# A new order for the jobs of the first 45 attention steps and of the first wide pair in a fused threshold attention and ELU feed-forward kernel

## The chip, the cores and the metric

The kernel runs on one core of a Trainium2 chip. The metric is the device time of one execution in microseconds (us); several executions of a kernel are timed, and the median is used. A profile is one more execution, recorded by the hardware profiler; its span runs from the first to the last instruction on the core.

The core has five engines that run side by side, each with its own queue, in order: TensorE (PE in the profile: matrix products; PEld is its loading of the stationary operand), VectorE (DVE), ScalarE (ACT), GpSimd (POOL) and SyncE (SP, which here only starts transfers, called DMAs). An instruction that needs another engine's result waits for a semaphore, and everything behind it on its own engine waits with it.

## The reference

```
def _attn_ref(q, k, v, tau):               # q, k, v: 8 batches, 8 heads, 576 positions, 64 channels
    scale = 1.0 / np.sqrt(q.shape[-1])
    scores = scale * np.matmul(q, k.transpose(0, 1, 3, 2))
    thresh = np.max(scores, axis=-1, keepdims=True) - tau
    scores = np.where(scores >= thresh, scores, -1000000000.0)
    scores = scores - np.max(scores, axis=-1, keepdims=True)
    attn = np.exp(scores)
    attn = attn / (np.sum(attn, axis=-1, keepdims=True) + 1e-09)
    return np.matmul(attn, v).astype(np.float32)

x = attn_out.transpose(0, 2, 1, 3).reshape(4608, 512)
h = x @ w_in                               # w_in: 512 x 2048
g = np.where(h > 0.0, h, np.exp(np.minimum(h, 0.0)) - 1.0)
out = g @ w_out                            # w_out: 2048 x 512
```

All is in float32, except the two weight matrices, which come as float64 and are turned into float32 on the core.

## The kernel before

**The work.** Attention goes by pairs of heads, 32 pairs in all, four to a batch. A pair has five blocks of queries: four of 128 queries for both heads (i = 0 to 3), and a last one that holds the remaining 64 queries of both heads (i = 4, named NC in the code). One block of one pair is a step. The first 45 steps are numbered n = 0 to 44: steps 0 to 7 are blocks 0 and 1 of pairs 0 to 3, steps 8 to 19 are blocks 2, 3 and 4 of pairs 0 to 3, and then each of the pairs 4 to 8 has five steps in a row (pair 8: steps 40 to 44). They are built by `early_tasks`. From pair 9 on (`JOINED`) a different, wider form is used (`wide_step`, `tail_step`); pair 9 is the first wide pair, and its stage has the letter "j". The feed-forward layer fills PE between the attention's matmuls: two half batches in a plain form within the 45 steps (`ffn1`, `ffn2_plain`, called halves), and the rest in a form with seven products in place of eight (`first_product`, `second_round`) beside and after the wide pairs.

**One step** is a chain over four engines, for each head h:

- `sc`: PE computes the scores into a bank of PSUM (line 650).
- `max`: DVE takes the negated row maximum (line 707).
- Then one of two forms. The plain form: `th` is the threshold on POOL (line 711), `exp` is exp(score - max) on ACT (line 745), and `mask` on DVE multiplies it by score >= threshold and sums the row (line 752). The sunk form, for the (step, head) pairs in `MASK_ACT`: `th` is on DVE (line 723), `exp` is a Prelu with a slope of 2^126 on ACT that sends what is below the threshold far down (line 730), and `mask` is an exp on ACT with the row sum (line 736). The bank of scores becomes free behind `mask` in the plain form and behind `exp` in the sunk one.
- `su`, `rec`: the row sum on DVE (line 760) or, for the steps in `SU_ACT`, on ACT (line 697), and its reciprocal on DVE (line 766).
- `norm`: the weights are divided by their sum: on POOL (line 703), on ACT for `ACT_NORM` (line 691), on DVE for `NORM_DVE` (line 686).
- The weights are transposed in one of two ways. `part` and `put`: PE transposes into PSUM in two or three parts (line 769), and each is copied out by ACT or, for `PUT_DVE`, by DVE (line 785). Or, for the steps named by `SQUARES` (most of 22 to 44): `turned`, DVE transposes 32 x 32 squares (line 845), SP writes them to DRAM with four DMAs (line 870), and `landed` is the DMA that fetches them back in the right order (line 878 or 887).
- `val`, `out`: PE multiplies by the values for two or three steps of a pair at once (lines 902 and 907), and ACT copies the result out.

**Other jobs** stand between the steps: `load`, `v`, `loadr` (DMAs of q, k, v; `loadr` brings the last 320 positions of pair 0's q), `prep`, `scale`, `copy` (q and k are transposed by DVE, line 561 and 569, and q is scaled on POOL), `rest` with nothing behind it (the transposition of what `loadr` brought, on DVE), and for each of 32 pieces of the weights `lw` (its DMA), `shift` (DVE line 478, or POOL line 476 for `SHIFT_POOL`), `rest` (ACT line 469, or POOL line 489 for `REST_POOL`), `sign` (ACT line 494), `add` (POOL line 484) and `end` (DVE line 502), which turn float64 into float32. `in` makes sums of weight blocks for the seven-product form, on DVE or POOL (`IN_POOL`). `half` and `post` are the feed-forward halves and what follows them: exp on ACT, minus one on POOL, the ELU on DVE; for a unit in `ELU_ACT`, ACT also makes the relu, and POOL does the rest with two instructions.

**Idle transposes** are transposes of the identity whose result nobody reads. 22 run at the start (line 1309, `idle(22)`), 16 beside step 0 (line 1549, `idle(16)`), and `IDLES` holds triples (step, part, count): so many are issued ahead of that part of that step, in the same PSUM tile.

**What sets the order.** Nothing is scheduled by the compiler: instructions stand on each engine in the order in which the Python code issues them. Each job has a due time made of a formula, a shift from the table `MOVED` for its kind, and a shift from `MOVED` for this one job. Jobs are issued in the order of due time; a job that needs others issues those first.

```
    def task(x, t, key, f, *needed):
        each = "_".join(map(str, x)) if isinstance(x, tuple) else x
        made[x] = [t + (MOVED.get(key, 0.0) if key else 0.0) + MOVED.get(each, 0.0), len(made), f, needed, False]

    def do(x):
        job = made[x]
        if not job[4]:
            job[4] = True
            for y in job[3]:
                if y:
                    do(y)
            job[2]()
...
        for x in sorted(made, key=lambda x: made[x][:2]):
            do(x)
```

So a due time far behind (1100, say) only means that the job is issued when another needs it. In the wide pairs, posts stand on an agenda with due times of their own, shifted by `MOVED` under keys that begin with the stage's letter.

Of the kernel before, what the change touches and what calls it, by code (L numbers as in the profile page):

```python
# [18 lines left out]
ACT_NORM = {(1, 1), (4, 1), (8, 0), (8, 1), (10, 0), (11, 0), (11, 1), (13, 0), (14, 1), (15, 0), (16, 0), (17, 0), (18, 0),  # L19
 (18, 1), (20, 0), (20, 1), (21, 0), (21, 1), (25, 0), (26, 0), (29, 0), (30, 0), (31, 0), (35, 0), (36, 0), (37, 0), (38,  # L20
 0), (40, 0), (42, 1), (43, 0), (44, 0)}
IN_POOL = {(0, 0), (1, 0), (1, 2), (2, 2), (3, 1), (4, 0), (4, 1), (4, 2), (5, 1), (5, 2), (6, 0), (6, 1), (6, 2), (7, 1),
 (7, 2)}
SU_ACT = {0, 2, 5, 7, 16, 17, 20, 21, 23, 24, 25, 27, 30, 33, 37, 38, 43, 44}
QK_PE = set()
MASK_ACT = {(0, 0), (0, 1), (1, 1), (2, 0), (5, 1), (7, 1), (8, 0), (9, 1), (12, 1), (13, 0), (15, 1), (16, 0), (17, 1),
 (20, 0), (20, 1), (23, 0), (23, 1), (24, 0), (25, 0), (25, 1), (26, 0), (26, 1), (27, 0), (27, 1), (28, 0), (29, 0), (30,
 0), (31, 0), (32, 0), (32, 1), (33, 0), (33, 1), (35, 1), (36, 1), (37, 0), (37, 1), (38, 1), (39, 0), (40, 0), (41, 0),
 (42, 0), (44, 0)}
SHIFT_POOL = {0, 2, 3, 19, 23, 24, 26, 29}  # L30
REST_POOL = {0, 2, 3, 4, 5, 7, 11, 12, 13, 17, 24, 27, 30, 31}
IDLES = {(0, 1, 1), (1, 2, 2), (2, 0, 3), (2, 2, 2), (3, 0, 5), (3, 1, 3), (3, 2, 3), (5, 0, 6), (5, 1, 4), (6, 1, 6), (7,
 0, 2), (7, 1, 2)}
ELU_ACT = {(1, 0), (1, 2), (1, 3), (1, 4)}
NORM_DVE = {(1, 0), (12, 0), (19, 0), (23, 0), (23, 1), (27, 0), (30, 1), (32, 0), (32, 1), (33, 0), (34, 0), (35, 1), (36,
 1)}
WIDE_ACT = {(9, 1, 0), (9, 2, 1), (9, 4, 0)}
PUT_DVE = {(0, 2), (4, 2), (6, 2), (10, 1), (11, 0), (11, 1), (11, 2), (12, 0), (12, 1), (12, 2), (14, 0), (18, 1), (20, 1),
 (21, 0), (26, 2)}

MOVED = {
# [322 lines left out]
def kernel(  # L364
# [921 lines left out]
    def early_tasks():  # L1286
# [159 lines left out]
        for n in range(MIDDLE):  # L1446
# [9 lines left out]
            if n == LATE:  # L1456
                task("switch", t, None, switch, *rooms)
            rooms += [("exp" if (n, h) in MASK_ACT else "mask", n, h) for h in hs]
            at_ = (lambda a, b, c=0: t + c) if last_ else (lambda a, b, c=0: t + b) if late_ else (lambda a, b, c=0: t + a)
# [606 lines left out]
```

## Time and profile before

| what | us |
|---|---|
| median of 3 runs (lowest, highest) | 1289.68 (1289.25, 1290.15) |
| the profiled execution's own time | 1287.79 |
| its span | 1286.0 |
| granted clock of PE, mean | 0.999 |

The page gives, for each engine, the time in which it was busy, and for stretches of the span the same, with the granted clock of PE (1.00 is full speed) and the share of the 16 DMA engines that was in use. Two things are needed to read it. A matmul's record is longer than the distance to the next, since they overlap: a float32 matmul with 256 columns is two passes that each show about 380 ns, while the next pass starts 216 ns later. So "busy" on PE includes short waits; what PE really had to do is counted by the undisturbed distance between starts. And a wait for several semaphores is put down to the one that came last by the records, which can be the wrong one when a DMA is among them.

The 45 steps end at about 270 us: the last early instruction of PE starts at 269.28 us.

### The profile page before, as it was taken

The page shows a single profiled execution, that of the slowest core. Times are in us where ns is not written, and L with a number is a line of the kernel's source. Part 1 is how long each engine was busy: PE and PEld are TensorE (multiplying, and loading weights), DVE is VectorE, ACT ScalarE, POOL GpSimd, SP SyncE. Part 2 cuts the span into 40 slices and gives each one's busy share as a digit, 9 for nine tenths or more (in the row PEclk, how much of TensorE's full clock was granted, in tenths as well). Part 3 has the DMA queues.
Part 4 walks back from the last instruction along what each step waited for, and adds up shares of the span by engine and source line. Part 5 has one row for each costly group of instructions (what it writes and reads, how often), then busy time and mean ns, then how long its engine had stood idle before and what let it go on. Part 6 is the DMA issues. An engine that isn't in the chain of part 4 may idle for free.

```text
span 1286.0 us, 21531 instructions
## 1 busy us (share of the span) xinstructions
PE 1268.9 (99%) x6749; PEld 986.9 (77%) x6749; DVE 997.8 (78%) x2145; ACT 598.0 (46%) x1298; POOL 792.8 (62%) x1149
## 2 busy tenths in 40 slices
PE   8999999999999999999999999999999999999998
PEld 6675575467778787888888787878787888888887
DVE  6797777779798988898889888997989872545534
ACT  6889775555352526253535444443535251421320
POOL 4777566587476847675676657674758473534523
PEclk9999999999999999999999999999999999999999
DMA  7467687988989998998989898989898874222221
GB/s 140 137 179 166 160 246 210 240 236 246 238 227 267 246 240 231 236 256 228 248 229 271 214 238 216 260 223 242 235 254 248 242 214 174 76 74 65 92 62 33
DMA packets 329586, 258.35 MB, mean 201 GB/s; under 512 B 209536, under 2 KB 290432, under 8 KB 329472
## 3 DMA queue, kind: packets, MB, share of 16 engines
q1 hardware_dynamic: 327376, 256.50, 73.7%
q8 instruction: 53, 0.87, 0.3%
q10 hardware_dynamic: 2096, 0.48, 0.2%
q14 instruction: 61, 0.50, 0.1%
HBM read 167.12 MB, written 89.78 MB: 200 GB/s over the span
## 4 chain that ended last, share of the span: by engine, by line
PE 87%; DVE 4%; DMA 3%; SPq 1%; POOL 1%; ACT 1%; issue 1%; DVEq 0%; ACTq 0%; POOLq 0%
PE f L1793 30%; PE f L1653 29%; PE sc L954 7%; PE sc L1027 7%; PE f L1079 4%; PE sc L650 3%; PE pv L907 2%; PE rt L769 2%; DMA there<-x 1%; PE sc L1019 1%; PE f L1131 1%; PE sc L1014 1%; DVE mx L707 1%; DMA wst<-in_moe_w_out_dram 1%; SPq L528 1%
## 5 line engine op out<-in xcount | busy, mean ns | idle before, releaser
L703 POOL TENSOR_SCALAR w<-w,rs 128x576 f32<-128x576 f32 x152 | 122.6, 816 | 81.1 <-DVE rs L766 71.8
L961 DVE TENSOR_REDUCE mx<-sc 128x1 f32<-128x576 f32 x207 | 148.1, 749 | 27.5 <-PE sc L954 23.7
L981 ACT ACTIVATE w<-sc,mx 128x576 f32<-128x576 f32 x113 | 81.6, 740 | 114.8 <-DVE mx L961 98.0
L1653 PE MATMUL f<-xt,sw 128*128 128x256 f32 x512 | 124.2, 385 | 1.5 <-ACT g L1715 0.5
L1653 PE MATMUL f<-xt,w_in_sb 128*128 128x256 f32 x512 | 122.3, 381 | 0.5 <-ACT w L1667 0.5
L845 DVE STREAM_TRANSPOSE x<-w 128x512 f32<-128x512 f32 (+1 forms) x153 | 108.9, 744 | 14.9 <-POOL w L703 11.9
L973 POOL TENSOR_SCALAR th<-mx,ntau 128x2 f32<-128x2 f32 (+1 forms) x114 | 35.0, 307 | 131.9 <-DVE mx L961 131.9
L1653 PEld LDWEIGHTS f<-xt,sw 128*128 128x128 f32 x512 | 93.5, 190 | 22.2 <-issue 4.5
L1653 PEld LDWEIGHTS f<-xt,w_in_sb 128*128 128x128 f32 x512 | 96.2, 190 | 16.1 <-ACT w L1667 3.2
L1793 PE MATMUL f<-w_out_sb,g 128*128 128x256 f32 x448 | 107.1, 382 | 0.0
L1793 PE MATMUL f<-w_out_sb,s 128*128 128x256 f32 x448 | 107.0, 382 | 0.0
L1653 PE MATMUL f<-x,w_in_sb 128*128 128x256 f32 x448 | 105.9, 379 | 0.0
L1793 PE MATMUL f<-t,s 128*128 128x256 f32 x448 | 105.8, 379 | 0.0
L954 PE MATMUL sc<-kT,qT 64*128 64x448 f32 (+4 forms) x736 | 103.4, 416 | 0.0
L954 PEld LDWEIGHTS sc<-kT,qT 64*128 64x128 f32 x736 | 80.7, 186 | 25.2 <-issue 16.2
L1740 POOL TENSOR_TENSOR s<-g 128x256 f32<-128x256 f32 x104 | 80.7, 781 | 28.5 <-PE f L1793 20.1
L988 DVE SCALAR_TENSOR_TENSOR w<-sc,th,w 128x576 f32<-128x576 f32 x113 | 88.1, 809 | 10.2 <-ACT w L981 9.9
L1793 PEld LDWEIGHTS f<-w_out_sb,g 128*128 128x128 f32 x448 | 84.1, 190 | 14.0 <-issue 3.1
L1793 PEld LDWEIGHTS f<-w_out_sb,s 128*128 128x128 f32 x448 | 84.1, 190 | 13.6 <-issue 2.5
L1653 PEld LDWEIGHTS f<-x,w_in_sb 128*128 128x128 f32 x448 | 85.0, 190 | 11.8 <-ACT s L1667 0.3
L1793 PEld LDWEIGHTS f<-t,s 128*128 128x128 f32 x448 | 85.1, 190 | 11.6
L703 POOL TENSOR_SCALAR e<-e,rs 128x576 f32<-128x576 f32 x92 | 68.1, 744 | 34.9 <-DVE rs L766 33.6
(232 smaller groups left out, 2858.0 us busy)
## 6 DMA issues: line engine op xcount, KB each, us to landing
there<-x SPq DMA_DIRECT2D x444, 144.0 KB, 3.8
wTb<-there SPq DMA_DIRECT2D x58, 576.0 KB, 6.1
wTa<-there SPq DMA_DIRECT2D x53, 576.0 KB, 5.1
sw<-win_sums SPq DMA_DIRECT2D x62, 384.0 KB, 4.1
t<-wout_sums SPq DMA_DIRECT2D x45, 512.0 KB, 5.6
qm<-in_q_dram SPq DMA_DIRECT2D x124, 72.0 KB, 4.9
wst<-in_moe_w_in_dram SPq DMA_DIRECT2D x16, 512.0 KB, 4.6
vm<-in_v_dram SPq DMA_DIRECT2D x64, 128.0 KB, 4.0
```

Of the source, the lines that this page charges most:

```text
L650: nc.tensor.matmul(scs[h][:, a, :HALF], qs[r], kT[r, k0 : k0 + HALF], start=True, stop=True)
L703: nc.gpsimd.tensor_scalar(wv, wv, st["rs"][:, h : h + 1], 1.0, ALU.mult, ALU.mult)
L845: nc.vector.transpose(x[:, :, c0 : c0 + nc_], src.rearrange("p (c g n) -> p g c n", c=nc_, n=T))
L954: on_banks(nc.tensor.matmul(o, qT[r, i * P : (i + 1) * P], kT[r, k0 : k0 + n], start=True, stop=True, skip_group_check=True), o)
L961: on_banks(nc.vector.tensor_reduce(st["mx"][:, h : h + 1], st["sc", h], axis=AX.XY if i == NC else AX.X, op=ALU.max, negate=True), st["sc" ...
L981: on_banks(nc.scalar.activation(st["e", h], st["sc", h], AF.Exp, bias=st["mx"][:, h : h + 1]), st["sc", h])
L988: on_banks(nc.vector.scalar_tensor_tensor(st["e", h], st["sc", h], st["th"][:, h : h + 1], st["e", h], ALU.is_ge, ALU.mult, accum_out=st[" ...
L1027: on_banks(nc.tensor.matmul(o, vm[:, h, c], parts[part][:, g0:g1, h * (NC + 1) + c], start=False, stop=(c == NC - 1), skip_group_check=Tru ...
L1079: nc.tensor.matmul(loc["ph"][:, k], w_in_sb[:, j, ft * P : (ft + 1) * P], xts[g][:, j, hf * CT : (hf + 1) * CT], start=(j == 0), stop=(j = ...
L1653: nc.tensor.matmul(loc["banks"][place], left[:, j], right[:, j], start=(begins and j == 0), stop=(j == 1), skip_group_check=True)
L1740: engine.tensor_tensor(o, x, y, op)
L1793: nc.tensor.matmul(place(m), lhs, rhs, start=(begins and v == 0), stop=(v == RU - 1), skip_group_check=True)
```

## The change

Only tables change: which engine does a job for which step, how many idle transposes there are, and the due times. The sets, as they stand in the diff:

```diff
-ACT_NORM = {(1, 1), (4, 1), (8, 0), (8, 1), (10, 0), (11, 0), (11, 1), (13, 0), (14, 1), (15, 0), (16, 0), (17, 0), (18, 0),
- (18, 1), (20, 0), (20, 1), (21, 0), (21, 1), (25, 0), (26, 0), (29, 0), (30, 0), (31, 0), (35, 0), (36, 0), (37, 0), (38,
- 0), (40, 0), (42, 1), (43, 0), (44, 0)}
-IN_POOL = {(0, 0), (1, 0), (1, 2), (2, 2), (3, 1), (4, 0), (4, 1), (4, 2), (5, 1), (5, 2), (6, 0), (6, 1), (6, 2), (7, 1),
- (7, 2)}
-SU_ACT = {0, 2, 5, 7, 16, 17, 20, 21, 23, 24, 25, 27, 30, 33, 37, 38, 43, 44}
+ACT_NORM = {(4, 1), (8, 0), (8, 1), (10, 0), (11, 0), (11, 1), (12, 0), (13, 0), (14, 1), (15, 0), (16, 0), (17, 0), (18,
+ 0), (18, 1), (20, 0), (20, 1), (21, 0), (21, 1), (25, 0), (26, 0), (28, 1), (29, 0), (35, 0), (36, 0), (37, 0), (38, 0),
+ (40, 1), (42, 0), (42, 1), (43, 0), (44, 0)}
+IN_POOL = {(0, 0), (0, 1), (1, 0), (1, 1), (2, 0), (2, 2), (3, 2), (4, 2), (5, 2), (6, 1), (6, 2), (7, 0), (7, 1)}
+SU_ACT = {0, 2, 15, 16, 17, 20, 23, 24, 25, 27, 32, 33, 35, 37, 43, 44}
...
-SHIFT_POOL = {0, 2, 3, 19, 23, 24, 26, 29}
-REST_POOL = {0, 2, 3, 4, 5, 7, 11, 12, 13, 17, 24, 27, 30, 31}
-IDLES = {(0, 1, 1), (1, 2, 2), (2, 0, 3), (2, 2, 2), (3, 0, 5), (3, 1, 3), (3, 2, 3), (5, 0, 6), (5, 1, 4), (6, 1, 6), (7,
- 0, 2), (7, 1, 2)}
-ELU_ACT = {(1, 0), (1, 2), (1, 3), (1, 4)}
-NORM_DVE = {(1, 0), (12, 0), (19, 0), (23, 0), (23, 1), (27, 0), (30, 1), (32, 0), (32, 1), (33, 0), (34, 0), (35, 1), (36,
+SHIFT_POOL = {2, 3, 16, 21, 23, 24, 28, 29, 30, 31}
+REST_POOL = {0, 1, 2, 3, 4, 5, 7, 10, 11, 12, 13, 17, 18, 24, 26, 27, 28, 30, 31}
+IDLES = {(1, 2, 1), (2, 0, 2), (2, 2, 2), (3, 0, 3), (4, 2, 2), (5, 1, 3), (6, 1, 4), (6, 2, 1), (7, 0, 1), (7, 1, 1)}
+ELU_ACT = {(1, 0), (1, 4), (1, 5)}
+NORM_DVE = {(1, 0), (5, 1), (17, 1), (19, 0), (22, 0), (23, 0), (23, 1), (28, 0), (32, 1), (33, 0), (34, 0), (35, 1), (36,
  1)}
-PUT_DVE = {(0, 2), (4, 2), (6, 2), (10, 1), (11, 0), (11, 1), (11, 2), (12, 0), (12, 1), (12, 2), (14, 0), (18, 1), (20, 1),
- (21, 0), (26, 2)}
+PUT_DVE = {(0, 1), (4, 2), (6, 2), (10, 1), (11, 0), (11, 2), (12, 1), (12, 2), (14, 0), (16, 1), (18, 1), (20, 0), (21, 0),
+ (26, 2)}
```

`MASK_ACT` gains (15, 0), (30, 1), (31, 1), (34, 0), (38, 0), (43, 0) and loses (31, 0), (36, 1), (39, 0): 45 sunk heads, not 42. The triples of `IDLES` add up to 20, not 39; the 22 and the 16 stay.

In `MOVED`, nearly every single-job shift of the 45 steps differs (203 of `post`, 100 of `rest`, 81 of `max`, 80 of `exp` and so on), and 121 of the keys of stage "j"; the shifts by kind of job and the keys of the other wide pairs ("s", "f") are the same. A few of the lines:

```diff
-    "add_0": -0.9, "add_1": 12.1, "add_10": 607.6, "add_11": 274.8, "add_12": 709.4, "add_13": 511.6, "add_14": 334.2,
+    "add_0": -13.9, "add_1": 13.1, "add_10": 700.6, "add_11": 219.8, "add_12": 675.4, "add_13": 494.6, "add_14":
...
```

What the new due times do to the order of the instructions, as far as it is spoken of later: `loadr` stands on SP right behind the first `lw`, ahead of pair 1's q and k, instead of behind pair 2's k; on DVE, `shift` of piece 0 and the transposition of the rest of q stand ahead of `max` of step 1, instead of on POOL and behind `rec` of step 3; `prep` of pair 2's q stands ahead of `mask` (2, 1) instead of behind it; between `rec` of step 12 and `rec` of step 14 DVE has three jobs fewer, which ACT has; on SP, the four DMAs of pair 9's k stand behind the writes of `turned` 41 and ahead of `landed` 40 and 41, instead of ahead of `turned` 38. On PE the order of the steps' matmuls stays the same from step 10 on, but for some feed-forward halves that stand one place earlier or later; in steps 0 to 9 `part` (3, 2) stands ahead of the scores of step 5 and `part` (4, 0) behind them as before.

More of the change, by code (lines that the diff above doesn't have):

```diff
@@ L25 @@
-QK_PE = set()
[L26 to L29, printed above, removed]
-SHIFT_POOL = {0, 2, 3, 19, 23, 24, 26, 29}
-REST_POOL = {0, 2, 3, 4, 5, 7, 11, 12, 13, 17, 24, 27, 30, 31}
@@ new lines @@
+IN_POOL = {(0, 0), (0, 1), (1, 0), (1, 1), (2, 0), (2, 2), (3, 2), (4, 2), (5, 2), (6, 1), (6, 2), (7, 0), (7, 1)}
+SU_ACT = {0, 2, 15, 16, 17, 20, 23, 24, 25, 27, 32, 33, 35, 37, 43, 44}
+QK_PE = set()
+MASK_ACT = {(0, 0), (0, 1), (1, 1), (2, 0), (5, 1), (7, 1), (8, 0), (9, 1), (12, 1), (13, 0), (15, 0), (15, 1), (16, 0),
[3 rows of a table added]
+SHIFT_POOL = {2, 3, 16, 21, 23, 24, 28, 29, 30, 31}
+REST_POOL = {0, 1, 2, 3, 4, 5, 7, 10, 11, 12, 13, 17, 18, 24, 26, 27, 28, 30, 31}
+IDLES = {(1, 2, 1), (2, 0, 2), (2, 2, 2), (3, 0, 3), (4, 2, 2), (5, 1, 3), (6, 1, 4), (6, 2, 1), (7, 0, 1), (7, 1, 1)}
```

609 rows, old and new, of tables (MASK_ACT, MOVED) are left out of this document.

## The prediction

> **What bounds the kernel.** I read the busy times, then windows cut at step boundaries, then what DVE and PE wait for in each.
>
> ```profile
> PE 1268.9 (99%) x6749; PEld 986.9 (77%) x6749; DVE 997.8 (78%) x2145; ACT 598.0 (46%) x1298; POOL 792.8 (62%) x1149
> ```
>
> PE bounds the whole. But its records overlap, so "busy" hides short waits. Counted by undisturbed distances between starts (109 ns for a 128x128 transpose, 216 ns for each pass of 256 columns), PE has 1204.3 us of work in the span of 1286.0 and is idle for 81.7. The change can win only from this, and touches the first 312 us. By window (columns: us, then PE, PEld, DVE, ACT, POOL busy, PEclk, DMA share, GB/s):
>
> ```profile
> 13.60:52.40 38.80, 37.40 (x261) 25.22 (x260) 31.35 (x74) 32.73 (x65) 26.34 (x43) 1.00 0.62 141
> 52.40:85.40 33.00, 32.12 (x183) 23.68 (x182) 30.43 (x66) 27.48 (x57) 25.15 (x29) 1.00 0.54 154
> 85.40:226.00 140.60, 139.60 (x665) 87.96 (x664) 108.02 (x225) 104.57 (x220) 91.83 (x115) 1.00 0.75 197
> 226.00:272.00 46.00, 41.56 (x175) 20.36 (x174) 36.02 (x75) 25.39 (x51) 30.87 (x47) 1.00 0.89 243
> ```
>
> PE's own idle time in these is 9.0, 2.95, 11.95 and 10.67 us (8.4 before 13.6, 6.7 in 272 to 312, 32.0 behind). So in the first two rows other engines set the pace for part of the time, in the third PE does, and in the fourth the DMAs (share 0.89) hold it. In the first row DVE leads: ACT's exps start 0.03 to 0.1 us behind DVE's maxima, while DVE waits for 7.45 us in all, most of it for
>
> ```profile
> DVE mx L707 <- PE sc L650: 2.7, 3, 1.4
> DVE w L752 <- ACT e L745: 2.5, 3, 1.3
> ```
>
> The second row's DVE is the tightest of all: from 61.2 to 85.5 us I find no wait of DVE's.
>
> **The change, term by term.** Over all, at this trace's durations, PE loses 19 transposes x 109 ns = 2.07 us; ACT 2.07 net (five `rest` of weights go to POOL, 3.43; three more sunk masks come, 2.33); DVE 1.14 net; POOL gains 0.49. None of this is a gain by itself; what counts is where it stood.
>
> *1. Steps 0 to 10.* Two of DVE's waits get work:
>
> ```profile
> 11.13 0.76 DVE L707 TENSOR_REDUCE mx<-sc 128x1 f32<-128x576 f32 x1 [1.19 <-PE sc L650]
> ...
> 19.69 0.82 DVE L752 SCALAR_TENSOR_TENSOR w<-sc,th,e 128x576 f32<-128x576 f32 x1 [0.90 <-ACT e L745]
> ```
>
> Into the first gap (1.19) go `shift` 0 (0.43) and the rest of q (0.51), which stood at 25.69 in the chain; into the second (0.90) `prep` of pair 2's q (0.78), which stood ahead of `max` (3, 0). The first needs `loadr`'s data by 10.6. Its four issues now stand right behind the first `lw`, where SP is idle from 4.22 to 5.82; at this trace's 2.60 us for four they go out from about 4.2 to 6.8, and `qr` lands 2.6 us after issue (median): 9.4, some 1.2 early. Pair 1's q and k go out that much later less SP's 1.6 of idle time; k had about 1.0 to spare. I follow the chain by hand: `max` (3, 0) 21.12 to about 20.4; `max` (4, 0) 26.16 to 25.3; `sc` (6) 34.27 to 33.05; `max` (8, 0) 43.68 to 42.45; `sc` (10) 52.40 to 51.2. Against it stand 1.6 us more of DVE work by step 10 (`norm` (5, 1), `put` (0, 1), two row sums), inside the 7.45 of waits; if that cover were gone, each would push its successor by itself (0.16 to 0.68). The idle transposes are not added: the five ahead of `part` (3, 0) end at 26.64 where `norm` on POOL ends at 26.59, and behind the six ahead of `part` (5, 0) PE still waits 0.23; without them most of that time becomes a wait. **1.2 us**; ends 0 and 2.1 (all transposes on the path).
>
> *2. Steps 11 to 15.* `put` (11, 1) (0.68), `put` (12, 0) (0.68) and `norm` (12, 0) (0.52) leave DVE for ACT, 1.88 us where DVE has no wait; ACT is free for 1.61 of 76 to 80 us. DVE could come 1.88 earlier, but PE can give back only its idle time between `sc` (10) and `sc` (15), 3.06, less the third row's steady 8% (about 1.0). **1.4**; ends 0 and 1.9.
>
> *3. 85 to 226 us.* PE is at 92% of what it could do. Two waits stand out, each for a POOL copy: 0.74 us at
>
> ```profile
> 144.29 1.24 PE L650 MATMUL sc<-kT,qd 128*128 128x288 f32 x4 [0.57 <-POOL qd L603]
> ```
>
> and 0.44 at `sc` (25). POOL gets 1.7 to 2.8 more work ahead of them (`rest`, `shift`) and has 2.19 and 2.79 idle there; DVE loses two shifts. **0.5**; ends -1.0 (POOL's cover fails) and 1.2 (both waits go).
>
> *4. 226 to 272 us.* These two rows decide:
>
> ```profile
> 262.50 1.21 PE L650 MATMUL sc<-kT,qd 128*128 128x288 f32 x4 [1.03 <-DVE w L752]
> ...
> 267.12 0.67 PE L902 MATMUL pv<-wTa,vd 128*128 128x256 f32 x2 [1.70 <-ACT w L730]
> ```
>
> `sc` (44) waits for `mask` (43, 0) on DVE; sunk, its bank is free behind `exp` on ACT, so that 1.2 goes. But `val` (8, 0) comes next. The row blames ACT, whose instruction was long done; `landed` 41 was issued at 261.53 and took 5.5 to 267.0, so the DMA holds it, and whatever `sc` (44) wins is waited here instead. Ahead of that issue the change puts pair 9's four loads of k (2.03 us for four in this trace), where SP has 1.07 + 0.80 = 1.87 idle:
>
> ```profile
> 254.10 4.73 SPq L870 DMA_DIRECT2D there<-x  x8
> 259.90 0.34 SPq L878 DMA_DIRECT2D wTa<-there  x1
> 260.29 0.43 SPq L1044 DMA_DIRECT2D xtail<-xs  x1
> 261.53 0.32 SPq L878 DMA_DIRECT2D wTa<-there  x1
> ```
>
> So nothing is lost at that price, and 2.0 of issues leave the way of `turned` 38 and 39. **0.2**; ends -1.3 (nothing gained above, the loads slow the landing) and 1.2.
>
> *5. The first wide pair.* The same jobs at other times; its PE waits add to 3.5 us (0.3 to 0.7 each). No row prices a reorder, so **0**, ends -1.5 and 1.5. The ELU unit takes 0.59 from ACT and 2.55 from POOL and gives DVE 0.68, with no PE instruction, inside POOL's 38%: 0.
>
> Sum: 1.2 + 1.4 + 0.5 + 0.2 + 0 = 3.3 us. On the profiled execution 1287.79 - 3.3 = 1284.5; the median of the runs is 1.89 above that one, so **1289.68 - 3.3 = 1286.4**, 0.26% faster. About 0.2%, 2.58 us, can be told from no change.
>
> **Rivals.**
>
> *B, the gain is given back (1287.1 to 1292.3, likeliest 1289).* PE arrives earlier and waits for what has not moved: `val` (7, 0), (7, 1) and (8, 0) wait 0.98, 0.59 and 1.86 for DMAs with the DMA share at 0.89. For it: that row. Against it: SP's issues follow the engines, so DMAs of work that comes earlier also start earlier. The same result comes by the clock:
>
> ```profile
> 6.76:10.18 3.42, 1.81 (x12) 1.00 0.79 164
> 10.18:13.59 3.41, 3.41 (x14) 0.50 0.75 142
> 27.24:30.65 3.41, 3.31 (x20) 1.00 0.92 148
> ```
>
> (Columns: us, PE busy, PEclk, DMA share, GB/s.) A window with 1.81 us busy was followed by one at half clock. The thinnest later one is the third: 2.06 of work, 0.55 of it idle transposes. If it drops under the bar, the next runs at half: 2.71 of work there against 1.71 possible, 1.0 lost. One to three such windows leave a gain of 2.3 to 0.3.
>
> The Trainium skill (TensorE: Matmul & The Clock Gate, Part 4: PE-mode transpose) says that transposes do not count as work for the clock; by that, taking them away could cost no window, and this half of rival B would be empty. The trace speaks against it: 22 idle transposes from 1.48 us, and nothing else on PE, are followed by full clock at 6.76. The sum is 3.3 by either.
>
> *C, slower (1294.5).* The queue of SP: pair 9's loads stand ahead of `landed` 40 and 41. Issues of `turned` 39 took 2.45 and 1.91 us each (245.9, 248.9) when the queue was full. Four at 2.45 are 9.8, less 1.87 idle, 7.9 late, passed one for one to `val` (8, 0); less 3.1 gained ahead, 4.8 slower: 1289.68 + 4.8 = 1294.5. It makes the total slower from about 1.25 us an issue, and by over 0.2% from 1.9. For it: DMA at 0.89. Against it: pair 9's k took 0.5 an issue at 238.95 in the same stretch.
>
> **Chances.** Forecast 0.56 (1283 to 1287: terms 1 and 2 mostly there); B 0.24; C 0.20. Faster by over 0.2%: 0.56; within: 0.24; slower: 0.20. The favourable ends add to about 8 (2.1 + 1.9 + 1.2 + 1.2 + 1.5), 1281.8, rounded down for the runs' spread to 1281; above, B whole and C up to 1293.5, four fifths of its price.
>
> **What would show it.** DVE works on the rest of q before `max` (1, 0), with no wait for its DMA, and waits less than 7.45 us from 13.6 to 51; `sc` (10) starts near 51.2; `sc` (15) near 82.8 instead of 85.4; PEclk stays 1.00 behind 13.6; `sc` (24) and `sc` (25) wait under 1.18 together; `sc` (44) waits for nothing; pair 9's issues take 0.5 each and `val` (8, 0) starts near 264. Wrong it is if `loadr` lands behind 10.6 (term 1 goes), if PE finds ACT's `put` late at 76 to 82 (term 2), if half clock is granted anywhere behind 13.6 (B), or if `landed` 41 is issued later than 261.5 (C).

## The result, and the profile after

Five runs of each kernel on one chip: 1281.10 us (1280.39 to 1283.91) against 1289.68 (1286.71 to 1290.45). The ratio is 0.9942, 95% interval 0.9925 to 0.9959: 7.5 us faster, between 5.3 and 9.7. The forecast was 3.3. The profiled execution of the changed kernel took 1281.1, with a span of 1279.3. Beside the experiments the kernel before ran again, with medians of 1287.1 to 1288.6, so every experiment is read by its ratio to the runs of the kernel before that were made together with it. The profiled execution of one experiment (a4_chain36) ran at a clock of 0.85, so only its times are read.

The page's first line and the windows at the places shown of the kernel before (us, then PE, PEld, DVE, ACT, POOL busy, PEclk, DMA share, GB/s):

```profile
PE 1262.5 (99%) x6730; PEld 983.5 (77%) x6730; DVE 995.2 (78%) x2146; ACT 596.4 (47%) x1295; POOL 794.0 (62%) x1150
```

```profile
13.60:52.40 38.80, 35.07 (x236) 22.79 (x237) 32.74 (x78) 31.93 (x63) 26.55 (x42) 1.00 0.66 148
52.40:85.40 33.00, 33.00 (x188) 24.28 (x187) 28.57 (x64) 29.78 (x62) 26.83 (x32) 1.00 0.47 146
85.40:226.00 140.60, 140.20 (x677) 87.97 (x676) 109.69 (x229) 103.72 (x219) 94.81 (x117) 1.00 0.77 205
226.00:272.00 46.00, 42.56 (x184) 22.78 (x181) 34.31 (x74) 26.82 (x54) 33.55 (x48) 1.00 0.95 250
```

They say less than they seem to. The engines' totals are nearly the same, and the windows now hold other steps. The useful ruler is the start of the same PE instruction in both traces: from `sc` (10) to `val` (8, 0) each stretch of the table holds the same PE instructions by kind and number in both kernels (64, 116, 650, 46 and 108 of them), and up to `sc` (10) only the 19 idle transposes differ, so a shorter stretch is time that PE no longer loses. The experiments give many more traces of stretches they leave alone, so each difference below is between medians: of ten traces of the kernel before and its variants, whose edits lie in few of the stretches, and of three of the changed kernel and its variants (ranges in brackets).

| stretch, from start to start | before, us | after, us | difference | forecast |
|---|---|---|---|---|
| 0 to `sc` (10) | 52.10 (51.54-52.82) | 51.48 (51.04-51.59) | -0.62 | -1.2 |
| `sc` (10) to (12) | 12.71 (12.37-12.79) | 11.60 (11.60-11.60) | -1.11 | |
| `sc` (12) to (15) | 20.32 (20.29-20.79) | 20.16 (20.16-20.16) | -0.16 | -1.4 from (10) |
| `sc` (15) to (37) | 137.04 (136.64-137.88) | 136.02 (136.02-136.23) | -1.02 | -0.5 |
| `sc` (37) to (39) | 11.88 (11.07-11.89) | 10.74 (10.74-10.74) | -1.14 | |
| `sc` (39) to `val` (8, 0) | 32.27 (31.50-33.29) | 31.59 (31.57-31.72) | -0.68 | -0.2 from (37) |
| `val` (8, 0) to the last | 1015.13 (1013.72-1016.48) | 1014.59 (1013.44-1017.23) | within the scatter | 0 |

At `val` (8, 0) the changed kernel is 4.9 us ahead. The stretch behind it scatters by nearly 4 us between kernels whose order there is the same, so what it adds cannot be read from these traces. The difference from `sc` (39) to `val` (8, 0) lies within the scatter too: 31.57 to 31.72 after is inside 31.50 to 33.29 before. The others lie outside it, but for d1 in the first stretch, where part of its edit lies (51.54 against 51.04 to 51.59).

A wait of PE is counted below as the distance between two starts less the undisturbed one. The idle time in brackets on a line is as a rule 0.16 to 0.17 less, since the record before it overlaps.

Two waits of PE are gone that every trace with the old order there has. The first, of 1.05, is at `part` (10, 1). PE in the kernel before, then in the changed one (start, us, engine, line, operation; in brackets the idle time and what ended it):

```profile
64.74 0.41 PE L769 MATMUL rt<-ident,w 128*64 128x128 f32 x2 [0.88 <-ACT wTb L785]
```

```profile
62.89 0.38 PE L767 MATMUL rt<-ident,w 128*64 128x128 f32 x2
```

ACT's copy comes late because the exps of step 11 ahead of it wait for DVE's maxima, and DVE comes late because two of its instructions are slow. DVE and then POOL in the kernel before:

```profile
58.67 1.15 DVE L502 SCALAR_TENSOR_TENSOR w_in_sb<-wtop,wst 128x512 f32<-128x512 f32 x1 [0.82 <-POOL wtop L484]
59.85 1.40 DVE L478 TENSOR_SCALAR wtop<-wst 128x512 uint32<-128x512 uint32 x1
```

```profile
58.61 0.66 POOL L489 TENSOR_SCALAR wst<-wst 128x512 f32<-128x512 uint32 x1
59.23 1.73 POOL L484 TENSOR_TENSOR wtop<-wtop,wst 128x512 int32<-128x512 int32 x1
```

and DVE in the changed kernel, where POOL starts its add only at 58.95:

```profile
57.83 0.69 DVE L500 SCALAR_TENSOR_TENSOR w_in_sb<-wtop,wst 128x512 f32<-128x512 f32 x1 [0.82 <-POOL wtop L482]
58.56 0.43 DVE L476 TENSOR_SCALAR wtop<-wst 128x512 uint32<-128x512 uint32 x1
```

The same two instructions (`end` of piece 5, `shift` of piece 7) take 2.55 us beside POOL's `rest` 7 and `add` 6, and 1.12 without: 1.43 us in a chain at whose end PE waits 1.05.

The second is at `sc` (38), the scores of two heads by 64 rows each. Before, and after:

```profile
229.03 0.75 PE L650 MATMUL sc<-kT,qT 64*128 64x288 f32 x2
230.08 1.23 PE L650 MATMUL sc<-kT,qT 64*128 64x288 f32 x6 [0.29 <-ACT w L730]
```

```profile
225.41 1.24 PE L648 MATMUL sc<-kT,qT 64*128 64x288 f32 x8
```

Undisturbed, the two heads' products run side by side, all eight passes in 1.24, and the next matmul on PE starts 1.17 behind the first pass. Before, two passes of one head run alone, the other head's first pass starts 1.05 behind them, and the next matmul starts 2.21 behind the first pass (2.18 to 2.21 in the nine traces with the old order): 1.04 lost.

A smaller loss of this kind shows no idle time at all. Before and after, at `sc` (30):

```profile
176.34 1.53 PE L650 MATMUL sc<-kT,qT 64*128 64x288 f32 x8
```

```profile
173.69 1.24 PE L648 MATMUL sc<-kT,qT 64*128 64x288 f32 x8
```

Here the second head's passes start 0.3 behind the first's. At `sc` (30), (31) and (35) the next matmul starts 1.43 to 1.49 behind the first pass in all ten traces of before and its variants, and 1.17 in all three of the changed kernel: about 0.86 in all.

### The profile page after: what moved, and what is told of

Same layout as the page of the kernel before. It is cut to its first block, busy times and chain, and to the rows that moved or that the text cites. A ratio compares the mean times of both kernels' runs of the same rounds, so it can differ in the third digit from the quotient of the medians.

```text
span 1279.3 us, 21480 instructions
## 1 busy us (share of the span) xinstructions
PE 1262.5 (99%) x6730; PEld 983.5 (77%) x6730; DVE 995.2 (78%) x2146; ACT 596.4 (47%) x1295; POOL 794.0 (62%) x1150
## 4 chain that ended last, share of the span: by engine, by line
PE 90%; DVE 3%; ACT 2%; DMA 2%; SPq 1%; POOL 1%; issue 1%; DVEq 0%; ACTq 0%; POOLq 0%
PE f L1791 30%; PE f L1651 29%; PE sc L952 8%; PE sc L1025 7%; PE f L1077 3%; PE sc L648 3%; PE f L1129 3%; PE pv L905 2%; PE rt L767 2%; PE sc L1017 1%; PE sc L1012 1%; DVE x L843 1%; DMA there<-x 1%; PE pv L900 1%; DVE mx L705 1%
## 5 line engine op out<-in xcount | busy, mean ns | idle before, releaser
L952 PE MATMUL sc<-kT,qT 64*128 64x320 f32 (+3 forms) x736 | 102.6, 416 | 0.0
```

The lines of the kernel that those rows point to most:

```text
L952: on_banks(nc.tensor.matmul(o, qT[r, i * P : (i + 1) * P], kT[r, k0 : k0 + n], start=True, stop=True, skip_group_check=True), o)
```

## The experiments

Nine of them put one part of the change alone into the kernel before.

**a1_idles** and **c1_idles_back**: the 20 idle transposes in the kernel before, and the 39 in the changed one.

```diff
-IDLES = {(0, 1, 1), (1, 2, 2), (2, 0, 3), (2, 2, 2), (3, 0, 5), (3, 1, 3), (3, 2, 3), (5, 0, 6), (5, 1, 4), (6, 1, 6), (7, 0, 2), (7, 1, 2)}
+IDLES = {(1, 2, 1), (2, 0, 2), (2, 2, 2), (3, 0, 3), (4, 2, 2), (5, 1, 3), (6, 1, 4), (6, 2, 1), (7, 0, 1), (7, 1, 1)}
```

> The kernel before with the 20 idle transposes of the changed kernel in place of its 39, nothing else. Theory 1 (they stand where PE waits anyway): sc (10) starts 0 to 0.4 us earlier than before's 52.40, the whole is 0 to 0.4 us faster. Theory 2 (each one is on the path): sc (10) about 2.07 us earlier, the whole 2 us faster. Theory 3 (they hold up the clock): a window of PEclk 0.50 appears behind 13.6 us and sc (10) is 1 us or more later.

> The changed kernel with before's 39 idle transposes, nothing else. Theory 1 (they stand where PE waits anyway): sc (10) starts 0 to 0.5 us later than the changed kernel's 51.59, the whole is 0 to 0.5 us slower than the changed kernel. Theory 2 (on the path): sc (10) about 2 us later, the whole 2 us slower.

a1: ratio 1.0004 (0.9994 to 1.0013), `sc` (10) at 52.08. c1: ratio to the kernel before 0.9955 (0.9940 to 0.9969), `sc` (10) at 51.48 against the changed kernel's 51.59. Up to `sc` (10) the 2.07 us of transposes cost nothing in either kernel, as theory 1 has it. For the whole, a1 agrees; c1 was not run beside the changed kernel, and its 5.8 us against 7.5 leave both theories open, since the intervals overlap. With c1 most of the gain is there while all 39 transposes stay.

**c2_early**: `loadr`, `shift` 0, the rest of q and `prep` early.

```diff
-SHIFT_POOL = {0, 2, 3, 19, 23, 24, 26, 29}
+SHIFT_POOL = {2, 3, 19, 23, 24, 26, 29}
-"max_2_1": 430.3, "prep_q_2": 243.3, "rest": 28.5, "shift_0": -12.92,
+"max_2_1": 4.1, "prep_q_2": 3.2, "rest": 4.0, "shift_0": -10.62,
```

> The kernel before with the early part of the change alone: loadr right behind the first lw, shift of piece 0 on DVE and the rest of q ahead of max (1, 0), prep of pair 2's q ahead of mask (2, 1); idle transposes as before. Theory 1 (DVE's chain carries term 1): sc (10) starts 0.6 to 1.2 us earlier than 52.40, and the whole is as much faster. Theory 2 (the gain up to sc (10) came from the idle transposes): sc (10) starts 0 to 0.2 us earlier.

Ratio 1.0007 (0.9995 to 1.0018), `sc` (10) at 52.82: later than in any other trace, against both theories. `max` (3, 0) does start at 20.20, not 21.12. But the edit also pushed pair 2's k behind pair 0's v on SP (issued at 17.91, not 15.97), and DVE waits for it, all of its gain and more:

```profile
23.65 0.78 DVE L569 STREAM_TRANSPOSE kT<-km 128x576 f32<-128x576 f32 x1 [1.72 <-DMA km<-in_k_dram]
```

d1 below repeats it without that slip.

**a2_part10**: one piece of PE work into the wait at `part` (10, 1), where the changed kernel also has one.

```diff
-"post_11_2_0_1": 63.4, "rest_half_11_2_0": -4,
+"post_11_2_0_1": 66.0, "rest_half_11_2_0": -24.501,
```

> The kernel before with one piece of PE work moved: the second part of the feed-forward half (11, 2), 0.87 us, from ahead of part (10, 0) to between part (10, 0) and part (10, 1), where PE waits 1.05 us for put (9, 2) on ACT. Theory 1 (the gain between sc (10) and sc (15) is that wait, covered by reordering PE): sc (12) starts 0.8 to 1.0 us earlier than 65.08, sc (15) likewise, the whole about 0.9 us faster. Theory 2 (the prediction's: that stretch is bound by DVE's work without a wait): sc (12) comes earlier but sc (15) stays within 0.3 us of 85.37.

Ratio 1.0002 (0.9992 to 1.0011), `sc` (10) to (12) 12.70 as ever. Both theories miss: PE now reaches `part` (10, 0) 0.87 sooner and waits there 1.01, for `put` (9, 0) in the same chain on ACT.

```profile
61.93 0.66 PE L769 MATMUL rt<-ident,w 128*128 128x128 f32 x4 [0.85 <-ACT wTb L785]
```

So PE's order alone does not bring that gain: the wait goes to the next link of the same chain.

**a3_three**: the three jobs of term 2 on ACT.

```diff
 ACT_NORM +(12, 0); NORM_DVE -(12, 0); PUT_DVE -(11, 1), -(12, 0)
```

> The kernel before with put (11, 1), put (12, 0) and norm (12, 0) on ACT instead of DVE, nothing else. Theory 1 (PE does not wait for DVE there): sc (15) starts within 0.3 us of 85.37, the whole is the same. Theory 2 (the prediction's term 2): sc (15) starts about 1.4 us earlier, the whole is 1.4 us faster.

Ratio 1.0004 (0.9995 to 1.0014); `sc` (12) to (15) 20.79, 0.5 longer than the median. DVE is freed of 1.88 us and PE does not come earlier; `norm` (13, 0) on ACT, which waits for DVE's reciprocal, now comes late, and PE waits 0.69 ahead of `part` (13, 0). The reciprocal is late because DVE, now earlier, waits 0.37 and 0.73 for PE and then starts an `end` beside an `add` on POOL (76.85 to 78.13), which takes 1.80 where the same job took 0.69 before:

```profile
76.87 1.80 DVE L501 SCALAR_TENSOR_TENSOR w_in_sb<-wtop,wst 128x512 f32<-128x512 f32 x1
```

So a3 does not test the relief by itself. What speaks against term 2's mechanism is the table: the three jobs lie between `sc` (12) and `sc` (15), and that stretch is only 0.16 shorter in the changed kernel, which has moved them too.

**b3_pool**: the moves around the copies that `sc` (24) and (25) wait for.

```diff
 NORM_DVE +(22, 0); SHIFT_POOL +30, +31
```

> The kernel before with norm (22, 0) on DVE instead of POOL and the shifts of pieces 30 and 31 on POOL instead of DVE, as in the changed kernel, nothing else. Theory 1 (these moves take away PE's waits for POOL's copies): the waits at sc (24), 0.74, and sc (25), 0.44, fall under 0.3 together, sc (26) starts 0.8 to 1.2 us earlier than 156.88. Theory 2 (POOL has 2.2 us more to do there and the copies come later; the halves' order took the waits away): the waits stay or grow, sc (26) starts at 156.5 or later.

Ratio 0.9999 (0.9990 to 1.0009). The waits are 0.31 and 0.00, theory 1's numbers, but for another reason: in six of the nine traces with POOL's old order `sc` (24) waits only 0.16 too; 0.34, 0.63 and 0.74 are in the other three. The 0.74 on which term 3 was built comes and goes between executions. Inconclusive for the edit.

**a4_chain36**: step 36's chain.

```diff
 MASK_ACT -(36, 1); IN_POOL +(7, 0)
```

> The kernel before with mask (36, 1) on DVE in the plain form, not sunk, and the weight sum (7, 0) on POOL instead of DVE; PE's order unchanged. Theory 1 (sc (38)'s wait of 0.80 us for exp (37, 1) is the end of DVE's chain of step 36): that wait falls under 0.3 us and sc (39) starts 0.5 to 0.8 us earlier; of it val (7, 0), which waits for a DMA, keeps at least half. Theory 2 (it went because PE reaches sc (36) two halves earlier in the changed kernel): the wait stays at 0.7 to 0.9. Theory 3 (the prediction's rival B): it falls, and val (7, 0) waits as much longer, so sc (40) starts where it did, 241.1.

Ratio 0.9991 (0.9981 to 1.0000). That is 1.2 us, not clear of no change. Its waits are not known; d1 takes them up.

**b1_mask43**: `mask` (43, 0) sunk.

```diff
 MASK_ACT +(43, 0)
```

> The kernel before with mask (43, 0) sunk, so that the bank sc (44) needs is released by exp on ACT, nothing else. Theory 1 (the prediction's term 4): sc (44) starts about 1.2 us earlier than 262.50, val (8, 0) waits that much longer for the DMA landed 41 and starts within 0.3 us of 267.12; the whole is the same. Theory 2 (ACT's out (6, 1) or the mask, not the DMA, holds val (8, 0)): val (8, 0) starts about 1 us earlier and the whole is 1 us faster.

Ratio 1.0001 (0.9991 to 1.0011). `sc` (44) waits 0.80, still for an exp on ACT; in the other traces with `mask` (43, 0) on DVE it waits 0.75 to 1.59, so its part is within the scatter. `val` (8, 0) still waits 1.79, for a DMA. The whole is the same, as theory 1 had it.

**b2_loads**: pair 9's q and k on SP as in the changed kernel.

```diff
-"load_k_9": 799.2, "load_q_9": 873.4,
+"load_k_9": 985.7, "load_q_9": 806.4,
```

> The kernel before with the changed kernel's order on SP for pair 9's q and k alone: q ahead of turned 38, k behind turned 41 and ahead of landed 40 and 41. Theory 1 (the two groups of loads ahead of turned 39 had filled the queue): turned 39's four issues take under 2.5 us, not 5.4; landed 41 is issued 0.3 to 0.9 us earlier than 261.53 and val (8, 0) starts 0.3 to 1.0 us earlier; val (7, 1)'s wait changes by under 0.6. Theory 2 (rival C of the prediction): the four issues of k take 1.2 us or more each and val (8, 0) starts later than 267.1.

Ratio 1.0004 (0.9995 to 1.0014). SP (`turned` 39 at 245.51, `landed` 39, `turned` 40 and 41, then k):

```profile
245.51 1.92 SPq L870 DMA_DIRECT2D there<-x  x4
...
250.77 0.57 SPq L887 DMA_DIRECT2D wTb<-there  x1
251.68 5.91 SPq L870 DMA_DIRECT2D there<-x  x8
257.64 2.28 SPq L528 DMA_DIRECT2D km<-in_k_dram  x4
```

`turned` 39 takes 1.92, not 5.36, and k 0.57 an issue: rival C's price of 2.45 does not occur. `landed` 41 goes out 0.5 sooner (261.03), but `val` (8, 0) starts at 266.82, within the scatter. The jam was no loss that reached PE.

**b4_j**: all keys of stage "j" from the changed kernel.

```diff
-"j0.0": -12.91, "j1.0": -2.74, ...
+(the changed kernel's keys that begin with j)
```

> The kernel before with all keys of the first wide pair's stage j from the changed kernel, nothing else. Theory 1 (the times of stage j are worth what the two traces differ by behind val (8, 0)): val (8, 0) starts as before, 267.1, the waits of PE between 286 and 309 us fall by 1 us or more, and the whole is 1.0 to 1.5 us faster. Theory 2 (the gain there follows from the earlier steps handing over in another state): the waits stay within 0.4 us and the whole is the same.

Ratio 1.0003 (0.9994 to 1.0012): nothing, theory 2. The waits of PE that the view lists from 280 to 312 us add to 1.3 in both kernels.

**c3_better**: the changed kernel with `landed` 39 and pair 9's k moved on SP.

```diff
-"landed_39": 908.22, "load_k_9": 957.2,
+"landed_39": 865.72, "load_k_9": 976.7,
```

> The changed kernel with two moves on SP: landed 39 ahead of turned 40, and pair 9's four loads of k behind landed 41. Theory 1 (val (7, 1) waits 1.18 us because landed 39 is issued behind turned 40, and landed 40 and 41 share the DMA engines with the loads): val (7, 1)'s wait falls under 0.3 us, val (8, 0) starts 0.5 to 1.5 us earlier than 261.69, and the whole is 0.5 to 1.5 us faster than the changed kernel. Theory 2 (val (8, 0) is held by the landing of turned 41's writes, whatever stands between): val (7, 1) comes earlier, val (8, 0) stays within 0.3 us, the whole is the same as the changed kernel.

Ratio to the kernel before 0.9955 (0.9938 to 0.9972), as c1, which ran together with it: no sign that it is faster than the changed kernel. `val` (7, 1) waits 0.28, not 1.18, but PE then waits 0.82 at `sc` (44), where the changed kernel's trace shows no wait, and `val` (8, 0) waits for its DMA as before:

```profile
256.13 1.21 PE L648 MATMUL sc<-kT,qd 128*128 128x288 f32 x4 [0.65 <-issue]
257.17 1.88 PE L1129 MATMUL f<-w_out_sb,g 128*128 128x512 f32 x4
261.16 0.70 PE L900 MATMUL pv<-wTa,vd 128*128 128x256 f32 x2 [2.11 <-DMA wTa<-there]
```

But c1, which has the changed kernel's order on SP, shows the same: no idle time ahead of `val` (7, 1), and at `sc` (44)

```profile
256.77 1.21 PE L649 MATMUL sc<-kT,qd 128*128 128x288 f32 x4 [0.65 <-issue]
```

So the wait of 1.18 comes and goes by itself, and none of this is c3's doing. From `sc` (39) to `val` (8, 0) c3 takes 31.59 and the changed kernel 31.57.

**d1_three_causes**: the three chains together in the kernel before, PE's order untouched.

```diff
 SHIFT_POOL -0; MASK_ACT -(36, 1); IN_POOL -(6, 0), -(7, 2), +(7, 0)
-"in_6_0": 1316.4, "max_2_1": 430.3, "max_35_0": 1118.2, "max_36_0": 962, "max_36_1": 1057.5, "prep_q_2": 243.3, "rest": 28.5, "rest_7": 56.3, "shift_0": -12.92, "v_0": 115.5,
+"in_6_0": 708.9, "max_2_1": 4.1, "max_35_0": 712.6, "max_36_0": 712.5, "max_36_1": 712.1, "prep_q_2": 3.2, "rest": 4.0, "rest_7": 69.5, "shift_0": -10.62, "v_0": 113.35,
```

> The kernel before with three small edits in stretches that do not meet. (1) The early chain as in c2_early, with v of pair 0 left ahead of pair 2's loads, so that k of pair 2 is not pushed back. (2) On POOL, rest of piece 7 stands behind th (11, 0) instead of ahead of add 6, so that end of piece 5 and shift of piece 7 on DVE do not run beside it. (3) mask (36, 1) plain on DVE; weight sums (6, 0) and (7, 2) on DVE and (7, 0) on POOL, and max (36, 0) and (36, 1) ahead of (7, 2). PE's order and the 39 idle transposes stay. Theory 1 (what PE waits for is the end of chains over DVE, and these three are what carried the gain): (1) max (3, 0) and max (4, 0) 0.5 to 0.9 us earlier and sc (10) at 51.2 to 51.7; (2) end of piece 5 takes 0.7 and shift of piece 7 0.43, not 1.15 and 1.40, and PE's wait at part (10, 1), 1.05 to 1.17 in all traces of the kernel before, falls under 0.3; (3) the wait at sc (38), 0.77 to 0.80, falls under 0.3; sc (40) 2 to 2.7 us earlier than the kernel before, and the whole 1.5 to 2.7 us faster. Theory 2 (single edits are taken back by the next wait, and only the whole new order is faster): sc (40) within 1 us of the kernel before and the whole within 1 us. Theory 3 (PE's order carries it): the waits at part (10, 1) and sc (38) stay over 0.7.

Ratio 0.9992 (0.9983 to 1.0000), 1.0 us (0 to 2.2): not clear of no change, and less than theory 1's 1.5. Its parts, one by one:

(1) `sc` (10) at 51.54, 0.56 under the median and 0.25 under the earliest trace with the old order. But the first `max` of all, (0, 0), which no edit touches, already scatters from 7.66 to 8.27, and a stretch of half clock between 10 and 15 us, which some traces have (see the last section), counts too. From `max` (0, 0) to `sc` (10) three traces of the old order without half clock (a2, a3, b2) take 44.10 to 44.12, d1 43.78 and the changed kernel 43.32, both without it: the early chain alone makes 0.3 of 0.8, with 39 idle transposes.

(2) The collision moved instead of going. `add` 6 now starts at 57.76, and `end` 5 runs into it:

```profile
57.84 1.77 DVE L502 SCALAR_TENSOR_TENSOR w_in_sb<-wtop,wst 128x512 f32<-128x512 f32 x1 [0.83 <-POOL wtop L484]
59.65 0.43 DVE L478 TENSOR_SCALAR wtop<-wst 128x512 uint32<-128x512 uint32 x1
```

The two take 2.20 together, 0.35 less than 2.55, and the wait at `part` (10, 1) is 0.74, 0.31 to 0.43 less than in the other traces; `sc` (10) to (12) is 12.37, 0.34 less. The wait follows DVE's chain one for one, with PE's order as before.

(3) The wait at `sc` (38) is gone, and the next matmul starts 1.17 behind its first pass:

```profile
227.73 1.24 PE L650 MATMUL sc<-kT,qT 64*128 64x288 f32 x8
```

`sc` (37) to (39) is 11.07, 0.81 under the median; 0.30 has come back at `sc` (37), whose next matmul starts 1.47 behind its first pass. But `val` (7, 0), which waits for a DMA, waits 1.57 where the other nine show 0 to 1.46, and `sc` (40) starts at 239.28, 0.8 earlier than the median of the other nine (240.10), not 2 to 2.7: of 0.56 + 0.34 + 0.81 about half is given back there, as theory 2 says; one trace cannot tell that from the scatter of this wait.

## Why the prediction was right, and where it was wrong

*The sign* held. The range held only just, with a median of 1281.10 against its low end of 1281, and by luck, since that end was the sum of all favourable ends of five terms of which two were wrong in their mechanism. The size was 3.3 of 7.5 (5.3 to 9.7).

*Term 1 (1.2; measured 0.62, or 0.8 from `max` (0, 0)).* The mechanism, DVE's early chain, is shown in part by d1, 0.3 of it; the size was too large. `sc` (10) was put at 51.2 and lies at 51.5, and the 52.40 that it was taken from is itself 0.3 above the median of that kernel's traces. DVE's listed waits from 13.6 to 51.6 did fall, from 6.7 to 4.6. That idle transposes cover waits, and are worth nothing, was right up to `sc` (10) (a1, c1).

*Term 2 (1.4; measured 1.27).* Right in size by luck, through a wrong mechanism. The prediction took DVE's work at 73 to 77 us as what PE waits for; the stretch that holds it is 0.16 shorter, and moving that work alone gave nothing (a3). The gain lies ahead of it, at `part` (10, 1), a wait of 1.05 that the prediction's sum never named, behind a collision on DVE. Its step "61.2 to 85.5 us I find no wait of DVE's" was the misreading: an engine without a wait is not yet the one others wait for, and the 1.40 of a `shift` that mostly takes 0.43 was counted as work.

*Term 3 (0.5; measured 1.02).* From the wrong waits: the 0.74 was chance, and from `sc` (15) to `sc` (30), where `sc` (24) and (25) lie, the medians are 90.42 before and 90.33 after. The gain lies behind, from `sc` (30) to `sc` (37): 46.61 to 46.66 before, 45.69 to 45.92 after. About 0.86 of it is the late second head at `sc` (30), (31) and (35), which the sum did not name. Why that head starts late there was not tested.

*Term 4 (0.2; measured 1.82 from `sc` (37), of which 0.68 is within the scatter).* The step that failed is leaving `sc` (38) out: 1.04 of the 1.14 up to `sc` (39), taken away by step 36's chain (d1). What the term said of `mask` (43, 0) stands in so far as it gains nothing alone (b1). That the wait at `sc` (44) goes with it does not: of the four traces that have this mask sunk, b1, c1 and c3 wait there for 0.80 to 0.83, and the changed kernel alone for about 0.1. That pair 9's loads cost nothing stands too (b2).

*Term 5 (0).* Right for the keys alone (b4).

*Rival B* described most of the single edits: `part` (10, 0), `part` (13, 0) and perhaps `val` (7, 0) each took a wait over. It failed for the whole: the idle time ahead of `val` (8, 0) is 1.36 to 2.35 in the ten traces of before and its variants and 1.81 to 2.24 in the three of the changed kernel, so the DMA it waits for came earlier with the rest, as the prediction's argument against B had it. Its half on the clock did not come: in the changed kernel PE is busy for 2.32 of the 3.40 us from 27.2, where the prediction's thinnest window had 3.31, and full clock follows (us, PE busy, PEclk, DMA share, GB/s):

```profile
27.20:30.60 3.40, 2.32 (x17) 1.00 1.01 170
30.60:34.00 3.40, 3.40 (x28) 1.00 1.01 274
```

Nor is there a bar just above 1.81 us of busy time, as the prediction read from its first window. In b2_loads, with the same order up to there, a window that begins where full clock is first granted shows the same 1.81, and full clock follows:

```profile
7.36:10.77 3.41, 1.81 (x14) 1.00 0.86 139
10.77:14.18 3.41, 2.68 (x21) 1.00 0.56 115
```

That idle transposes count as work for the clock, as the prediction argued from its trace, c2_early shows more directly: full clock is granted at 4.26 us, before any other product has run on PE, and the distance between the idle transposes falls from 0.21 to 0.11 us there.

*Rival C* is refuted by 0.5 to 0.6 us an issue, in the changed kernel and in b2. Its price of 2.45 for each of four issues was too high from the start: of the four of `turned` 39 that it was read from two were slow (1.91 and 2.45), the others took 0.42 and 0.44.

**Open.** The traces show 4.9 us at `val` (8, 0), and the median spans of the same traces differ by 5.0 (1285.7 and 1280.7). The times show 7.5, and 5.8 in c1 and c3, whose own medians are 4.7 and 4.8 below that of the kernel before. What lies between was not located. And d1 has 1.8 of the 4.9 (it reaches `val` (8, 0) at 264.82, where the other nine do so from 265.30 to 267.97): the rest is shown by stretch, not by cause.

## What to carry to other kernels

Price a gain by the wait of the bounding engine and follow the chain behind it back to the instruction that took longer than its kind; a busy engine in between is no proof. Where two heads' products run side by side on PE, look at the distance from the first pass to the next matmul, since a late second head shows as busy time. Expect a single repair to move the wait to the next link, and judge a reorder by all links of a stretch at once. Before building on a wait of some tenths, or reading an experiment by one, see whether a second trace of the same kernel has it.

## What the runs showed that was not expected

**DVE and POOL block one another.** In the first 270 us of the kernel before, `shift`, `end`, `norm` and the weight sums on DVE take at most 0.43, 0.69, 0.52 and 0.42 when POOL is idle, and up to 1.40, 1.77, 1.41 and 0.95 beside it; `max` and `mask`, which read PSUM, stay at 0.76 and 0.82 either way. Counted above the shortest of each kind, the four lose 10.8 us before and 7.9 after. The Trainium skill (SBUF — State Buffer, Who interferes with whom) says that such instructions share a port with GpSimd and that the second to issue is blocked for the whole of the first. The trace agrees to 0.13 us: in d1, `add` 6 holds until 59.05 (57.76 + 1.29), 0.69 more is 59.74, and `end` 5 ends at 59.61.

**Half clock comes and goes.** Behind the start, one stretch of half clock of 3.41 us, between 9.9 and 14.9 us, is in 8 of 13 traces and in no other place, with the same instructions there or with others: the kernel before has it, the changed one not, c1 and c3 have it. Over the eight kernels whose early order is that of before (a1 with fewer idle transposes), `max` (0, 0) to `sc` (10) takes 44.32 to 44.51 in the five with it and 44.10 to 44.12 in the three without: 0.2 to 0.4 us. In the changed order it takes 43.32 without it and 43.65 and 43.36 with it (c1, c3), so the cost there is not settled. The Trainium skill (TensorE: Matmul & The Clock Gate, What's actually happening) has the clock's window run freely from before the kernel starts; that it comes and goes between executions agrees with this.
